# Q's and K's projections: weight columns streamed head by head, or with the two heads of a pair interleaved

## The chip, the cores and the metric

The kernel runs on one core of one Trainium2 chip. The core has a matrix engine (TensorE, "PE" in the profile, with its weight loads shown apart as "PEld"), a vector engine (DVE), a scalar engine (ACT), a GpSimd engine (POOL) and DMA queues that SyncE (SP) issues. Two memories on the chip matter here: SBUF, which holds operands, and PSUM, eight banks into which TensorE writes its products in float32. Both have 128 partitions. The metric is the time of one execution on the device, in microseconds (us). Before the change it was 845.99 us, the median of two runs (844.23 and 847.74).

## The reference

The input x has 2048 rows of 512. The output is a gated mix `g * a + (1 - g) * b`, where `g = sigmoid(sum(x * gate_w))`, `b` is a layer norm followed by a two-layer MLP with GELU (512 to 1376 to 512), and `a` is a recurrent attention over 64 segments of 32 rows, in order:

```
mem = mem0                                    # 8 rows of 512
for s in range(64):
    h = concat([mem, x[32*s : 32*s+32]])      # 40 rows
    q, k, v = h @ Wq, h @ Wk, h @ Wv          # 32 heads of 128 each
    p = softmax(mask(q @ k.T * scale))        # per head, 40 x 40
    o = (p @ v) @ Wo                          # back to 512
    mem = o[:8];  out[s] = o[8:]
```

Segment s+1 needs the memory rows that segment s ends with, so the segments form one chain from first to last.

## The kernel before, in words

The MLP runs first (lines 290 to 519, about the first 114 us of the span) and writes its part, already multiplied by `1 - g`, to DRAM. Then a loop of 64 segments follows (lines 600 to 669). Instructions stand in the order in which they are written: each engine works its own list from front to back, under a schedule that is written out by hand (`manual_schedule`).

A segment has 8 memory rows and 32 new rows. 24 of the new rows travel with the memory rows as a block of 32 rows (`hT`, three buffers used in turn). The other 8 rows of each of four segments are gathered into a second block of 32 rows (`GL`), and what is computed from it is computed ahead, for a tile T of four segments, in the gaps of earlier segments. The code calls these "left".

**The projections.** `qk_unit` (line 106) issues four matmuls for one of the four 128-row chunks `kc` of the model width. Each has 32 stationary columns (the 32 rows of the block) and streams 512 moving columns out of the weight matrix. The four, j = 0 to 3, go to four 32-column strips of the array (`tile_position=(0, 32 * j)`) and write the four groups of 32 partitions of one PSUM bank, so they run side by side; the text calls four such matmuls a quad. Strip j streams elements 32j to 32j+31 of each of 16 heads. A bank holds half of the heads (`hf`) of Q (`t` = 0) or K (`t` = 1), and takes four quads, 16 matmuls. A segment has four such banks `U[0]` to `U[3]` (Q and K, both halves, lines 615 to 623), 64 matmuls, and then V's eight quads (`v_unit`, line 126) into `X1` and `X2`.

`qk_cast` (line 112) turns a bank on ACT from float32 into a bf16 tile `Tb`. In `Tb` the two heads of a pair lie interleaved, so that two bf16 numbers form one 32-bit word. `qk_tr` (line 117) then transposes 32-bit words in blocks of 32 x 32 on DVE, into `QT` and `KT` (or `QL` for the left rows of Q; `kl_tr`, line 121, writes `KL` for the left rows of K). `scores` (line 249) multiplies them: `scores(s, 0)` uses the first half of the heads, `scores(s, 1)` the second. In the loop the order on TensorE is: 64 matmuls for Q and K, four quads of V into X1, two quads of V into X2, both halves of the scores, the last two quads of V.

After the scores come the exponentials on ACT (lines 636 and 637), the sums on TensorE (`sums`, line 263), a reciprocal and a multiplication on DVE (lines 647 and 648), the product with V (`av`, line 271), a copy to `UT` on ACT (line 653), the product with Wo (`wo_pass`, line 592, with line 140), a cast on ACT (line 596), a selection on TensorE (line 664) and the copy of the new memory rows into the next `hT` (line 665). Between these steps `run(n)` takes n quads from `side(T, si)`, the work for left rows. For `si` 0 and 1 these are the left rows of Q and K (`left_qk`, eight quads a segment), for `si` 3 those of V, for `si` 2 Wo of the left rows and the output. `W1`, `W2` and `W3` (line 599) set how many quads go into each gap: four before `av`, one after it, two after `wo_pass`, and the rest after line 664. `left_qk` hands its cast to a list `act_q` that is emptied behind the first bank of the next segment.

Of the kernel before, what the change touches and what calls it, by code (L numbers as in the profile page):

```python
# [27 lines left out]
def kernel(ctx, tc, A_x, A_mem0, A_Wq, A_Wk, A_Wv, A_Wo, A_seg_len, B_x, B_w1, B_b1, B_w2, B_b2, gate_w, out):  # L28
    nc = tc.nc
    P = 128  # L30
    _, S, Dm = A_x.shape
    H, Dh = A_Wq.shape[1], A_Wq.shape[2]
# [12 lines left out]
    NP = H // 2  # L45
# [12 lines left out]
    Wq_sb = pers.tile([P, KC, HD], BF16)  # L58
    Wk_sb = pers.tile([P, KC, HD], BF16)
# [37 lines left out]
    Sb = SbF[:, 0:NG * EW].rearrange("p (i c) -> p i c", c=EW)  # L97
    W = lps.tile([P, 512], FP32)

    Wq5 = Wq_sb[:].rearrange("p k (h j e) -> p k h j e", h=H, j=4)  # L100
    Wk5 = Wk_sb[:].rearrange("p k (h j e) -> p k h j e", h=H, j=4)
    W5 = (Wq5, Wk5)
    Wv5 = Wv_sb[:].rearrange("p k (i j e) -> p k i j e", i=NG, j=4)
    HF = ((0, H // 2), (H // 2, H))

    def qk_unit(bk, G, t, hf, kc):
        h0, h1 = HF[hf]
        for j in range(4):
            nc.tensor.matmul(bk[32 * j:32 * j + 32, :], lhsT=G[:, kc, :], rhs=W5[t][:, kc, h0:h1, j, :],  # L109
                             start=(kc == 0), stop=(kc == KC - 1), tile_position=(0, 32 * j))  # L110

    def qk_cast(bk):
        Tb = ew.tile([P, 8, 32, 2], BF16, tag="Tb", bufs=3, name="Tb")
        nc.scalar.copy(out=Tb[:].rearrange("p a e b -> p a b e"), in_=bk.rearrange("p (a b e) -> p a b e", a=8, b=2))  # L114
        return Tb

    def qk_tr(Tb, dst, hf):
# [52 lines left out]
    def left_qk(T, t, hf, bk):  # L170
        for kc in range(KC):
            qk_unit(bk, gl(T), t, hf, kc)
            if kc < KC - 1:
                yield
        def ca():
            Tb = qk_cast(bk[:])
            dve_q.append(lambda: qk_tr(Tb, QL[T % 2], hf) if t == 0 else kl_tr(Tb, T, hf))
        act_q.append(ca)
        yield
# [420 lines left out]
    for s in range(nseg):  # L600
# [14 lines left out]
        for n, (t, hf) in enumerate(((0, 0), (1, 0), (0, 1), (1, 1))):  # L615
            bk = U[n]
            for kc in range(KC):
                qk_unit(bk, hc, t, hf, kc)
            if n == 0:
                flush(act_q, 9)  # L620
            qk_tr(qk_cast(bk[:]), (QT, KT)[t], hf)
            if n == 0:
                flush(dve_q, 9)
# [209 lines left out]
```

## Time and profile before

| what | value |
|---|---|
| median of two runs | 845.99 us (844.23 to 847.74) |
| the profiled execution | 847.08 us, of which the span from first to last instruction 845.3 us |
| TensorE busy | 794.9 us (94%) |
| ACT busy | 559.5 us (66%) |
| DVE busy | 414.0 us (49%) |
| POOL busy | 252.2 us (30%) |
| granted TensorE clock, mean | 0.991 |
| line 109, Q and K matmuls | 4096 from `hT`, 1024 from `GL` |
| line 114, casts of Q and K | 258 from `U`, 62 from `X` |

Busy time is the time in which an engine has at least one instruction running. Matmuls are pipelined and their ends are modelled by the profile, so one matmul's shown duration (about 379 ns for 512 columns) is longer than the spacing of two; the spacing of starts is what counts. The "chain" is the work that ended last, followed back from the last instruction to what released each step. In the groups, the columns are: line, engine, operation, output and input, partitions x elements and type, count, then the busy time and the mean duration of one in ns, then the idle time of that engine just before. In the timeline, the columns are the start, the length, the engine, the line, the operation, and how many instructions are merged.

### The profile page before, as it was taken

How to read it: one execution, taken by the hardware profiler on the slowest of the kernel's cores; microseconds unless marked ns; L12 is line 12 of the kernel's file. 1: busy time of each engine (PE TensorE's matmuls, PEld its weight loads, DVE VectorE, ACT ScalarE, POOL GpSimd, SP SyncE). 2: the span in 40 equal slices, each digit the busy share in tenths (PEclk: the TensorE clock that was granted, in tenths of full speed). 3: DMA queues.
4: the chain of work that ended last, by engine and by line, in shares of the span. 5: the costliest groups of instructions: out<-in, count | busy, mean ns of one | idle time of the engine just before them, and what ended most of it. 6: DMA issues, size and time to landing. Idle time of an engine off the chain costs nothing.

```text
span 845.3 us, 39489 instructions
## 1 busy us (share of the span) xinstructions
PE 794.9 (94%) x17629; PEld 418.6 (50%) x17657; DVE 414.0 (49%) x942; ACT 559.5 (66%) x1311; POOL 252.2 (30%) x378
## 2 busy tenths in 40 slices
PE   2989999999999999999999999999999999999886
PEld 1656644555444545444445554444545454444443
DVE  5556435454445455544545454445445544544444
ACT  1545676676767676767676776767676767676663
POOL 3000013333333333333323333332333233323331
PEclk9989999999999999999999999999999999999999
DMA  9973011212122111212121212121111212121111
GB/s 294 414 281 122 27 40 46 72 54 78 53 72 66 56 58 58 78 60 78 53 85 51 62 53 83 54 77 61 60 54 60 78 59 78 59 72 52 57 51 61
DMA packets 39001, 70.30 MB, mean 83 GB/s; under 512 B 4005, under 2 KB 29194, under 8 KB 37290
## 3 DMA queue, kind: packets, MB, share of 16 engines
q1 hardware_dynamic: 38698, 67.59, 23.2%
q8 instruction: 140, 2.29, 1.1%
q0 software_dynamic: 128, 0.13, 0.2%
q14 instruction: 35, 0.29, 0.1%
HBM read 59.06 MB, written 4.45 MB: 75 GB/s over the span
## 4 chain that ended last, share of the span: by engine, by line
PE 75%; DVE 11%; ACT 8%; issue 3%; DMA 2%; SPq 1%; POOL 0%; DVEq 0%; ACTq 0%
PE U L109 27%; PE W L140 15%; PE X L128 13%; ACT w L596 4%; DVE R L647 3%; PE U L278 3%; ACT UT L653 2%; PE SbF L254 2%; PE U L460 2%; PE X L140 2%; PE W L664 2%; DVE E L648 2%; PE X L109 1%; PE U L265 1%; DMA xt<-in_A_x_dram 1%
## 5 line engine op out<-in xcount | busy, mean ns | idle before, releaser
L114 ACT CAST Tb<-U 128x512 bf16<-128x512 f32 x258 | 186.7, 761 | 64.6 <-PE U L109 38.7
L588 POOL TENSOR_TENSOR UT<-XR,Rb 128x768 bf16<-128x768 bf16 x63 | 105.0, 1667 | 253.8 <-DMA Rb<-r_dr 209.8
L109 PEld LDWEIGHTS <-hT 128*32 128x32 bf16 x4096 | 103.9, 97 | 116.7 <-DVE hT L665 15.7
L109 PE MATMUL U<-Wq_sb,hT 128*32 128x512 bf16 x2048 | 133.3, 380 | 5.7 <-DVE rmin L666 3.5
L128 PE MATMUL X<-Wv_sb,hT 128*32 128x512 bf16 x2048 | 132.8, 379 | 0.0
L109 PE MATMUL U<-Wk_sb,hT 128*32 128x512 bf16 x2048 | 132.7, 379 | 0.0
L140 PE MATMUL W<-Wo_sb,UT 128*32 128x512 bf16 x2080 | 124.1, 380 | 6.2 <-ACT UT L653 1.2
L118 DVE STREAM_TRANSPOSE QT<-Tb 128x256 f32<-128x256 f32 x128 | 57.0, 446 | 129.8 <-ACT Tb L114 126.8
L582 POOL TENSOR_TENSOR racc<-racc,R 128x320 f32<-128x320 f32 x63 | 54.6, 867 | 218.6 <-DVE R L577 210.7
L577 DVE RECIPROCAL R<-SbF 128x256 f32<-128x256 f32 x63 | 110.3, 1750 | 0.3 <-PE SbF L268 0.3
L140 PEld LDWEIGHTS <-UT 128*32 128x32 bf16 x2080 | 56.1, 96 | 60.6 <-issue 22.3
L653 ACT CAST UT<-U 128x64 bf16<-128x64 f32 x252 | 35.3, 226 | 69.9 <-PE U L283 69.9
L665 DVE CAST hT<-W 128x32 bf16<-128x32 f32 x63 | 12.1, 192 | 135.8 <-PE W L664 135.8
L572 ACT CAST XR<-U 128x256 bf16<-128x256 f32 x252 | 78.4, 434 | 0.0
L128 PEld LDWEIGHTS <-hT 128*32 128x32 bf16 x2048 | 49.9, 96 | 41.7
L118 DVE STREAM_TRANSPOSE KT<-Tb 128x256 f32<-128x256 f32 x128 | 56.8, 444 | 26.2 <-ACT Tb L114 25.8
L647 DVE RECIPROCAL R<-U 128x64 f32<-128x64 f32 x63 | 35.1, 558 | 69.7 <-PE U L268 66.4
L596 ACT CAST w<-W 128x512 bf16<-128x512 f32 x65 | 38.1, 586 | 44.5 <-PE W L140 44.5
L460 PE MATMUL U<-w_sb,hTm 128*128 128x512 bf16 (+1 forms) x164 | 51.6, 394 | 2.2 <-DMA w_sb<-in_B_w_dram 1.6
L454 PEld LDWEIGHTS <-w_sb 128*128 128x128 bf16 (+1 forms) x352 | 35.2, 104 | 32.5 <-issue 16.8
L114 ACT CAST Tb<-X 128x512 bf16<-128x512 f32 x62 | 46.3, 746 | 5.4 <-PE X L109 2.2
L109 PE MATMUL X<-Wk_sb,GL 128*32 128x512 bf16 x496 | 43.5, 384 | 0.0
(135 smaller groups left out, 1100.9 us busy)
## 6 DMA issues: line engine op xcount, KB each, us to landing
Rb<-r_dr SPq DMA_DIRECT2D x63, 512.0 KB
Wq_sb<-in_A_Wq_dram SPq DMA_DIRECT2D x4, 1024.0 KB
Wk_sb<-in_A_Wk_dram SPq DMA_DIRECT2D x4, 1024.0 KB
Wv_sb<-in_A_Wv_dram SPq DMA_DIRECT2D x4, 1024.0 KB
Wo_sb<-in_A_Wo_dram SPq DMA_DIRECT2D x4, 1024.0 KB
VP<-VL SPq DMA_DIRECT2D x64, 64.0 KB
xt<-in_A_x_dram SPq DMA_DIRECT2D x16, 128.0 KB
c_dr<-ct SPq DMA_DIRECT2D x16, 128.0 KB
```

Source lines behind the costliest of these rows:

```text
L109: nc.tensor.matmul(bk[32 * j:32 * j + 32, :], lhsT=G[:, kc, :], rhs=W5[t][:, kc, h0:h1, j, :], start=(kc == 0), stop=(kc == KC - 1), tile_ ...
L114: nc.scalar.copy(out=Tb[:].rearrange("p a e b -> p a b e"), in_=bk.rearrange("p (a b e) -> p a b e", a=8, b=2))
L118: nc.vector.transpose(out=dst[:, 8 * hf:8 * hf + 8, 0:32, :].rearrange("p a r b -> p a (r b)").bitcast(FP32), in_=Tb[:].rearrange("p a e b ...
L128: nc.tensor.matmul(bk[32 * j:32 * j + 32, :], lhsT=G[:, kc, :], rhs=Wv5[:, kc, 4 * vb:4 * vb + 4, j, :], start=(kc == 0), stop=(kc == KC - ...
L140: nc.tensor.matmul(bk[32 * c:32 * c + 32, :], lhsT=U_[:, j, i, :], rhs=Wo_sb[:, 4 * i + j, :], start=(n == 0), stop=(n == NW - 1), tile_po ...
L460: nc.tensor.matmul(bp(blk, tt)[:], lhsT=hTm[blk % 2][:rows, fc, tt * P:(tt + 1) * P], rhs=w2_sb[:rows, fc, :], start=(fc == 0), stop=(fc = ...
L572: nc.scalar.copy(out=XR[:, j], in_=U[j][:, 0:NG * 40].rearrange("p (i q) -> p i q", q=40)[:, :, 8:40])
L577: nc.vector.reciprocal(out=R[:, 8 * NG:], in_=SbF[:, 0:32 * NG])
L582: nc.gpsimd.tensor_tensor(out=racc[:], in0=racc[:], in1=R[:], op=ALU.add)
L588: nc.gpsimd.tensor_tensor(out=UT[(s + 1) % 2][:].rearrange("p j i q -> p (j i) q")[:, :, M:32], in0=XR[:, :, 0:RIDE], in1=Rb[:, :, 0:RIDE] ...
L596: nc.scalar.copy(out=w[:], in_=W[:])
L647: nc.vector.reciprocal(out=R[:, 0:8 * NG], in_=U[0][:, 320:384])
```

## The change

Three lines of the set-up and one of the cast change. The views `Wq5` and `Wk5` of the weights now give, for strip j, the order (pair a, element e, head b of the pair) instead of (head, element): the weights stay where they are in SBUF, but the moving operand takes element e of the first head, element e of the second head, then element e+1 of the first, and so on. `HF` counts pairs instead of heads. The columns of the PSUM bank come out in that order, so the cast reads and writes in order. V's view (`Wv5`) and all else stay.

```diff
-    Wq5 = Wq_sb[:].rearrange("p k (h j e) -> p k h j e", h=H, j=4)
-    Wk5 = Wk_sb[:].rearrange("p k (h j e) -> p k h j e", h=H, j=4)
+    Wq5 = Wq_sb[:].rearrange("p k (a b j e) -> p k a e b j", b=2, j=4, e=32)
+    Wk5 = Wk_sb[:].rearrange("p k (a b j e) -> p k a e b j", b=2, j=4, e=32)
     W5 = (Wq5, Wk5)
     Wv5 = Wv_sb[:].rearrange("p k (i j e) -> p k i j e", i=NG, j=4)
-    HF = ((0, H // 2), (H // 2, H))
+    HF = ((0, NP // 2), (NP // 2, NP))
 
     def qk_unit(bk, G, t, hf, kc):
         h0, h1 = HF[hf]
         for j in range(4):
-            nc.tensor.matmul(bk[32 * j:32 * j + 32, :], lhsT=G[:, kc, :], rhs=W5[t][:, kc, h0:h1, j, :],
+            nc.tensor.matmul(bk[32 * j:32 * j + 32, :], lhsT=G[:, kc, :], rhs=W5[t][:, kc, h0:h1, :, :, j],
                              start=(kc == 0), stop=(kc == KC - 1), tile_position=(0, 32 * j))
 
     def qk_cast(bk):
         Tb = ew.tile([P, 8, 32, 2], BF16, tag="Tb", bufs=3, name="Tb")
-        nc.scalar.copy(out=Tb[:].rearrange("p a e b -> p a b e"), in_=bk.rearrange("p (a b e) -> p a b e", a=8, b=2))
+        nc.scalar.copy(out=Tb[:].rearrange("p a e b -> p (a e b)"), in_=bk)
         return Tb
```

## The prediction

> **What bounds the kernel now.** I read the page's chain first, to learn which engine sets the end, then the timeline of one segment, then the groups by form for the durations.
>
> ```profile
> PE 75%; DVE 11%; ACT 8%; issue 3%; DMA 2%; SPq 1%; POOL 0%; DVEq 0%; ACTq 0%
> ...
> L114 ACT CAST Tb<-U 128x512 bf16<-128x512 f32 x258 | 186.7, 761 | 64.6 <-PE U L109 38.7
> ...
> L109 PE MATMUL U<-Wq_sb,hT 128*32 128x512 bf16 x2048 | 133.3, 380 | 5.7 <-DVE rmin L666 3.5
> ```
>
> TensorE holds 75% of the chain, and the largest entry of the chain by line is L109, the Q and K matmuls, with 27%. The L114 casts are not in the chain by name, though they are ACT's largest group. So the edit touches two things of unlike weight: the matmuls that bound the kernel, and a cast beside them. The timeline of a segment without Q/K left work (TensorE, and the last K transposition on DVE):
>
> ```profile
> 429.83 1.05 PE L109 MATMUL U<-Wq_sb,hT 128*32 128x512 bf16 x16
> 430.71 1.04 PE L109 MATMUL U<-Wk_sb,hT 128*32 128x512 bf16 x16
> ...
> 433.30 1.47 PE L128 MATMUL X<-Wv_sb,hT 128*32 128x512 bf16 x24
> 434.59 0.27 PE L254 MATMUL SbF<-QT,KT 128*32 128x40 bf16 x16
> 434.70 0.20 PE L258 MATMUL SbF<-QT,KL 128*32 128x64 bf16 x4
> 434.82 0.28 PE L254 MATMUL SbF<-QT,KT 128*32 128x40 bf16 x16
> ```
> ```profile
> 434.32 0.45 DVE L118 STREAM_TRANSPOSE KT<-Tb 128x256 f32<-128x256 f32 x1 [0.37 <-ACT Tb L114]
> ```
>
> The 64 matmuls start at 429.83 and V's first at 433.30: 3.47 us (3.46 in the segment from 406.93 to 410.39, which I use), or 0.216 us for a quad, 54 ns a matmul. V's 24 take 1.29 us to the next start, 54 ns too. A quad streams four times 512 columns in 0.216 us, so any change in how fast columns come reaches the time directly.
>
> The last K transposition ends at 434.77, and the second half of the scores starts at 434.82. The first half's L258 had started at 434.70, and a quad of 64 columns takes 0.03 us (the same quad at 434.94 is followed by V's at 434.96). So about 0.09 us of every segment is a wait for the last cast and transposition, although TensorE shows no idle time there.
>
> **Part one, the cast.** Rows by form:
>
> ```profile
> L596 ACT CAST w<-W 128x512 bf16<-128x512 f32 x65 | 38.1, 586 | 44.5 <-PE W L140 44.5
> ...
> L124 DVE STREAM_TRANSPOSE KL<-Tb 128x128 f32<-128x128 f32 x64 | 19.9, 391 | 3.0 <-ACT Tb L114 3.0
> ...
> L118 DVE STREAM_TRANSPOSE QL<-Tb 128x256 f32<-128x256 f32 x32 | 13.0, 405 | 7.2 <-ACT Tb L114 7.2
> ...
> L409 DVE TENSOR_TENSOR nt<-rs 128x2 f32<-128x2 f32 x24 | 3.9, 161 | 0.8
> ```
>
> L596 is the same cast in order, 512 float32 of PSUM to bf16: 586 ns. The 320 L114 casts (761 and 746 ns) should become that, some 171 ns less each, 55 us of ACT's 559.5 us. Nearly all of it lies beside TensorE's next quads. What reaches the path is the 0.09 us above, since the last cast's saving of 0.17 us is larger than that wait: 64 x 0.09 = 5.8 us gained. Behind it the exponential (L636) waits for the scores, with ACT idle 0.23 us ahead of it, so it does move up.
>
> **Part two, the moving operand.** No instruction is added, no DMA, no wait; the 5120 L109 matmuls read in another order. Before, a strip reads runs of 32 neighbouring elements (64 bytes). After, it alternates between two places 256 bytes apart and moves on by 2 bytes every second element. No matmul in this trace reads like that. The nearest on TensorE is L258, whose elements are 4 bytes apart, at the full rate (a quad of 64 columns in 0.03 us, by starts). That is one end: no cost. The nearest row with a wide step is on another engine: L124 writes words 512 bytes apart, L118 in runs. With the 161 ns of L409's two elements as the fixed part, L118 costs (405 - 161) / 256 = 0.95 ns a word and L124 (391 - 161) / 128 = 1.80 ns: 1.9 times. With the extreme durations of these groups (375 and 421 ns for L124, 401 and 446 for L118, the latter also into QT) it is 1.5 to 2.2 times. The worst end: the four strips of a quad take turns. One 512-column matmul alone takes 0.216 us (two of L460 take 0.43 in the chain), so a quad would take 0.864 us, 4 times.
>
> I take 2 times: the widest-step row gives 1.9, and a stream that loses one turn per element loses a whole one.
>
> [...]
>
> Path at 2 times. Main banks: 3.46 us more a segment, x 64 = 221.4 us, all on the chain. Left banks: eight quads in each of 30 segments (si 0 and 1, T + 1 from 1 to 15). They sit in gaps:
>
> ```profile
> 402.11 0.62 PE L109 MATMUL X<-Wq_sb,GL 128*32 128x512 bf16 x8
> 402.84 0.28 PE L278 MATMUL U<-E,V 32*128 32x40 bf16 x16
> ...
> 403.24 0.40 PE L109 MATMUL X<-Wk_sb,GL 128*32 128x512 bf16 x4
> 403.72 1.91 PE L140 MATMUL W<-Wo_sb,UT 128*32 128x512 bf16 x32
> ...
> 405.63 0.62 PE L109 MATMUL X<-Wk_sb,GL 128*32 128x512 bf16 x8
> 406.32 0.26 PE L664 MATMUL W<-SelM,w 128*128 128x8 bf16 x4
> ```
>
> From start to the next start less 0.216 us a quad, the free time is 0.30 us before L278 (four quads lie ahead of it), 0.26 before L140 (one), 0.26 before L664 (two), and 0.21 before the next segment (one quad from 406.50, L109 at 406.93). Doubled quads need 0.86, 0.22, 0.43 and 0.22 more; what sticks out is 0.56 + 0 + 0.17 + 0 = 0.73 us, x 30 = 21.9 us. The other 64 left matmuls run in the MLP's last block, 16 quads x 0.216 = 3.5 us. The cast gives back 5.8 us, since the cover of the last cast (six quads of V) does not change.
>
> Sum: 221.4 + 21.9 + 3.5 - 5.8 = 241.0 us, on the profiled execution's 847.08: 1088 us. That execution was 1.1 us over the median; I say **1087 us**, +28%.
>
> **Rivals.**
> *The strips also take turns (4 times).* For it: four streams at once now ask for a new place with every column. Against it: in the old order four strips together cost no more than one L460 matmul, and L258's four strips neither. Main 64 x 10.38 = 664.3; left, the four gaps need 2.59, 0.65, 1.30 and 0.65 more, 4.16 us net, x 30 = 124.8; first block 10.4; cast -5.8: 1641 us. Anything between 2 and 4 belongs here. [...]
> *The feed keeps its rate (not slower).* If whatever feeds a strip holds both places between accesses, or fetches fast enough for any step, part two is nothing and only the cast counts: 847.1 - 5.8 = 841 us, and no more, since the scores cannot start before the first half's L258 is through. The point is a quad of 0.222 us: above it the main banks' 64 x 16 quads lose more than the 5.8 us. For it: L258 at a step of 4 bytes. Against it: L124, and ACT's own L114, whose writes 4 bytes apart take 761 instead of 586 ns.
> *The cast doesn't get shorter.* Then each number is 5.8 us higher; it changes no verdict.
>
> **Numbers.** 0.58 for a loss of 1.5 to 2.2 times a quad; 0.22 for strips hindering each other as well; 0.16 for the full rate; 0.04 for something between or beyond. The first case's low end at 1.5 times: 110.7 + 3.9 + 1.7 - 5.8 = 110.5 us, 957 us. The range takes that and the turns' full price: 955 to 1640 us, which leaves out the full-rate case. A change under 2% (17 us) is hardly told from none here, so the full-rate case counts as "same": 0.13, with 0.03 for faster, should the cast free more than I see, and 0.84 for slower.
>
> **What would show it.** Right: starts of two L109 banks in a segment 1.73 us apart instead of 0.87; L109's share of the chain near 40%; L114 at about 586 ns; V's and Wo's quads still at 0.216 us; the granted clock as before; DVE and ACT idle longer ahead of L118 and L114. Wrong: banks 0.87 us apart (the feed does not mind), or 3.5 us (turns). A quad price that differs between Q and K, or between main and left banks, would say that the places in SBUF matter and not the step.

## The result, and the profile after

With the change an execution takes 1160.5 us (1160.03 and 1160.97), against 845.99 us before: 1.371 times as long, with a 95% interval of 1.367 to 1.375. The span of the profiled execution is 1159.2 us against 845.3, 313.9 us more. It was predicted to be slower, 1087 us in a range of 955 to 1640; the direction and the range held, and the loss was 73 us larger than the sum.

The page of the changed kernel: the chain by engine and by line, then the groups (line, engine, operation, count, busy us, mean ns, idle us before).

```profile
PE 89%; DVE 6%; ACT 3%; DMA 1%; issue 1%; SPq 0%; DVEq 0%
PE U L109 43%; PE X L109 11%; PE W L140 10%; PE X L128 10%; PE U L278 2%; ACT w L596 2%; PE U L460 2%; PE X L140 2%; PE SbF L254 1%; PE W L664 1%; PE U L265 1%; DVE R L647 1%; PE W L454 1%; DMA xt<-in_A_x_dram 1%; ACT UT L653 1%
...
L114 ACT CAST Tb<-U 128x512 bf16<-128x512 f32 x258 | 151.2, 586 | 361.6 <-PE U L109 361.1
L109 PE MATMUL U<-Wq_sb,hT 128*32 128x512 bf16 x2048 | 269.1, 644 | 1.4 <-DVE hT L665 1.1
...
L128 PE MATMUL X<-Wv_sb,hT 128*32 128x512 bf16 x2048 | 133.8, 379 | 0.0
```

The cast did what its edit says: 586 ns instead of 761. But ACT now stands idle for 361 us ahead of it, waiting for L109. L109 holds 43% of a longer chain, with another 11% for the left banks in X, where before it was 27% and about 1%. V's matmuls, whose view of the weights was not touched, took 133.8 us, against 132.8 before. So the loss is in Q's and K's matmuls. One segment on TensorE, with left work (the counterpart of the two timelines in the prediction):

```profile
571.13 2.11 PE L109 MATMUL U<-Wq_sb,hT 128*32 128x512 bf16 x16
573.07 2.10 PE L109 MATMUL U<-Wk_sb,hT 128*32 128x512 bf16 x16
...
578.86 1.47 PE L128 MATMUL X<-Wv_sb,hT 128*32 128x512 bf16 x24
...
580.25 0.20 PE L258 MATMUL SbF<-QT,KL 128*32 128x64 bf16 x4
580.28 0.31 PE L254 MATMUL SbF<-QT,KT 128*32 128x40 bf16 x16
...
583.28 0.27 PE L278 MATMUL U<-E,V 32*128 32x40 bf16 x16
...
584.17 1.90 PE L140 MATMUL W<-Wo_sb,UT 128*32 128x512 bf16 x32
...
587.15 0.25 PE L664 MATMUL W<-SelM,w 128*128 128x8 bf16 x4
...
587.83 2.10 PE L109 MATMUL U<-Wq_sb,hT 128*32 128x512 bf16 x16
```

A bank of 16 matmuls takes 1.93 us by starts (571.13 to 573.07 and on to 578.86), a quad 0.482 us instead of 0.216: 2.23 times. The four banks take 7.73 us instead of 3.47. The second half of the scores now starts 0.03 us after L258, where it was 0.12.

### The profile page after: what moved, and what is told of

Same layout as the page of the kernel before. It is cut to its first block, busy times and chain, and to the rows that moved or that the text cites. A ratio compares the mean times of both kernels' runs of the same rounds, so it can differ in the third digit from the quotient of the medians.

```text
span 1159.2 us, 39517 instructions
## 1 busy us (share of the span) xinstructions
PE 1122.0 (97%) x17657; PEld 413.7 (36%) x17657; DVE 417.4 (36%) x942; ACT 514.7 (44%) x1311; POOL 250.6 (22%) x378
## 4 chain that ended last, share of the span: by engine, by line
PE 89%; DVE 6%; ACT 3%; DMA 1%; issue 1%; SPq 0%; DVEq 0%
PE U L109 43%; PE X L109 11%; PE W L140 10%; PE X L128 10%; PE U L278 2%; ACT w L596 2%; PE U L460 2%; PE X L140 2%; PE SbF L254 1%; PE W L664 1%; PE U L265 1%; DVE R L647 1%; PE W L454 1%; DMA xt<-in_A_x_dram 1%; ACT UT L653 1%
## 5 line engine op out<-in xcount | busy, mean ns | idle before, releaser
L114 ACT CAST Tb<-U 128x512 bf16<-128x512 f32 x258 | 151.2, 586 | 361.6 <-PE U L109 361.1
L109 PE MATMUL U<-Wq_sb,hT 128*32 128x512 bf16 x2048 | 269.1, 644 | 1.4 <-DVE hT L665 1.1
L109 PE MATMUL U<-Wk_sb,hT 128*32 128x512 bf16 x2048 | 268.8, 644 | 0.0
L109 PEld LDWEIGHTS <-hT 128*32 128x32 bf16 x4096 | 105.3, 97 | 355.6 <-issue 339.4
L118 DVE STREAM_TRANSPOSE QT<-Tb 128x256 f32<-128x256 f32 x128 | 57.0, 445 | 265.9 <-ACT Tb L114 262.4
L128 PE MATMUL X<-Wv_sb,hT 128*32 128x512 bf16 x2048 | 133.8, 379 | 0.0
L140 PE MATMUL W<-Wo_sb,UT 128*32 128x512 bf16 x2080 | 123.8, 379 | 3.7 <-ACT UT L653 1.2
L118 DVE STREAM_TRANSPOSE KT<-Tb 128x256 f32<-128x256 f32 x128 | 57.0, 445 | 151.8 <-ACT Tb L114 151.8
L140 PEld LDWEIGHTS <-UT 128*32 128x32 bf16 x2080 | 54.3, 96 | 62.5 <-issue 22.3
L109 PE MATMUL X<-Wk_sb,GL 128*32 128x512 bf16 x496 | 75.9, 648 | 0.0
L109 PE MATMUL X<-Wq_sb,GL 128*32 128x512 bf16 x496 | 69.6, 644 | 0.0
L460 PE MATMUL U<-w_sb,hTm 128*128 128x512 bf16 (+1 forms) x176 | 54.6, 395 | 1.3 <-DMA w_sb<-in_B_w_dram 1.3
L114 ACT CAST Tb<-X 128x512 bf16<-128x512 f32 x62 | 36.5, 589 | 31.6 <-PE X L109 31.6
```

Of the source, the lines that this page charges most:

```text
L114: nc.scalar.copy(out=Tb[:].rearrange("p a e b -> p (a e b)"), in_=bk)
L118: nc.vector.transpose(out=dst[:, 8 * hf:8 * hf + 8, 0:32, :].rearrange("p a r b -> p a (r b)").bitcast(FP32), in_=Tb[:].rearrange("p a e b ...
L140: nc.tensor.matmul(bk[32 * c:32 * c + 32, :], lhsT=U_[:, j, i, :], rhs=Wo_sb[:, 4 * i + j, :], start=(n == 0), stop=(n == NW - 1), tile_po ...
L460: nc.tensor.matmul(bp(blk, tt)[:], lhsT=hTm[blk % 2][:rows, fc, tt * P:(tt + 1) * P], rhs=w2_sb[:rows, fc, :], start=(fc == 0), stop=(fc = ...
```

## The experiments

Each kernel ran next to the kernel before. Where no interval is given, the time is that of one execution, and the reading rests on the spacing of starts in its trace, which is the same in each segment.

### The cast alone

The matmuls as before, only the cast in order:

```diff
-        nc.scalar.copy(out=Tb[:].rearrange("p a e b -> p a b e"), in_=bk.rearrange("p (a b e) -> p a b e", a=8, b=2))
+        nc.scalar.copy(out=Tb[:].rearrange("p a e b -> p (a e b)"), in_=bk)
```

> The matmuls read as before the change; only the cast copies in order. The columns then reach Tb with the two heads of a pair not interleaved, so the scores mix other elements; the work is the same. Theory: the cast is worth 0.09 us a segment, the wait of the second half of the scores for the last transposition: 840 us (0.7% faster than before), L114 at 586 ns, the second L254 group 0.03 us after L258 instead of 0.12. Rival: the cast lies wholly beside other work: 846 us, ratio 1.000.

Measured: 843.14 us against 847.02, a ratio of 0.9957 (0.9940 to 0.9973). L114 fell to 586 ns. The timeline of one segment on TensorE:

```profile
556.63 0.20 PE L258 MATMUL SbF<-QT,KL 128*32 128x64 bf16 x4
556.66 0.31 PE L254 MATMUL SbF<-QT,KT 128*32 128x40 bf16 x16
556.79 0.22 PE L258 MATMUL SbF<-QT,KL 128*32 128x64 bf16 x4
```

The wait behind the first L258 is gone, as the theory said, so the cast was not wholly beside other work. It is worth less than the sum had it: the steps behind the wait each take about 0.01 to 0.02 us longer, so that from the first L258 to L265 it is 0.79 us (556.63 to 557.42) instead of 0.84 (434.70 to 435.54), and the segment (551.77 to 562.80) lasts 11.03 us instead of 11.09. From the loop's first matmul to the end it is 727.0 us (841.3 - 114.30) against 730.5 (845.3 - 114.76): 3.5 us, or 0.055 a segment, where 0.09 was expected.

### The moving operand alone

The matmuls as after the change, the cast as before it.

> The matmuls read as after the change; the cast writes at a 4-byte step as before it (so Tb gets the two heads in another order, and the scores mix other elements). Theory: the whole loss is the matmuls': 1160 us as with the change, or up to 6 us more; a bank of 16 matmuls takes 1.93 us by starts. Rival, that part of the loss comes from the two together: clearly under 1150 us.

Measured: 1160.57 us. Its groups:

```profile
L109 PE MATMUL U<-Wq_sb,hT 128*32 128x512 bf16 x2048 | 269.1, 644 | 1.4 <-DVE hT L665 1.1
...
L114 ACT CAST Tb<-U 128x512 bf16<-128x512 f32 x258 | 190.2, 737 | 328.8 <-PE U L109 328.4 <-ACT ct L466 0.4
```

L109's busy time is the changed kernel's to the tenth, with the slow cast beside it. The whole loss is the matmuls'. That the total is no larger than with the change is the first stage's doing: the loop starts at 116.63 us here and at 119.75 in the trace of the change. From there to the end it is 1042.2 us against 1039.5, so the fast cast is still worth 2.7 us.

### One strip of four

Is it the strips that hinder each other, or does each pay alone? Only strip 0 reads interleaved:

```diff
+    W6 = [W_[:].rearrange("p k (a b j e) -> p k a e b j", b=2, j=4, e=32) for W_ in (Wq_sb, Wk_sb)]
...
-            nc.tensor.matmul(..., rhs=W5[t][:, kc, h0:h1, j, :],
+            nc.tensor.matmul(..., rhs=W6[t][:, kc, h0 // 2:h1 // 2, :, :, j] if j < 1 else W5[t][:, kc, h0:h1, j, :],
```

> Only strip 0 of each quad reads with the two heads interleaved; strips 1 to 3 read runs of 32 elements; the cast copies in order (strips 1 to 3 so arrive not interleaved, and the scores mix other elements there). Theory A, each strip pays on its own: a quad takes as long as its slowest strip, between 0.43 and 0.48 us, so 1070 to 1155 us; a value below 0.48 gives the part of the 2.23 times that the four strips add to each other. Theory B, the strips share one feed and the penalties add up: a quad of 0.216 + 0.067 = 0.28 us, about 912 us.

Measured: 1160.23 us, as with four strips. The added line moves the matmuls to line 110. The timeline on TensorE:

```profile
558.11 0.40 PE L110 MATMUL U<-Wq_sb,hT 128*32 128x512 bf16 x3
558.58 0.64 PE L110 MATMUL U<-Wk_sb,hT 128*32 128x512 bf16 x1
558.59 0.40 PE L110 MATMUL U<-Wq_sb,hT 128*32 128x512 bf16 x3
559.06 0.64 PE L110 MATMUL U<-Wk_sb,hT 128*32 128x512 bf16 x1
```

One matmul of each quad is shown with 0.64 us, the other three with 0.40. The three even belong to a later bank: the strips drift apart, then all go on at the pace of the slow one, which comes every 0.48 us. So a strip alone needs 0.48 us for 512 interleaved columns, and three more interleaved strips add nothing to that. The rival in which the strips take turns is out, in part as well as in whole: all of the 2.23 times is one strip's own rate.

### How many elements in a row

Now the moving operand takes r neighbouring elements from each of 16 heads in turn, places 256 bytes apart; the cast is in order. The edit, with r = 1, 2 and 4 (32 is the kernel with the cast alone):

```diff
-    Wq5 = Wq_sb[:].rearrange("p k (h j e) -> p k h j e", h=H, j=4)
-    Wk5 = Wk_sb[:].rearrange("p k (h j e) -> p k h j e", h=H, j=4)
+    Wq5 = Wq_sb[:].rearrange("p k (h j e f) -> p k e h f j", h=H, j=4, f=r)
+    Wk5 = Wk_sb[:].rearrange("p k (h j e f) -> p k e h f j", h=H, j=4, f=r)
...
-            rhs=W5[t][:, kc, h0:h1, j, :]
+            rhs=W5[t][:, kc, :, h0:h1, :, j]
```

> The moving operand takes two neighbouring elements (4 bytes) from each of 16 heads in turn, places 256 bytes apart, then the next two; the cast copies in order (the scores mix other elements). [...] Theory B, each jump costs the same wherever it comes: half as many jumps as with the change, a quad of 0.216 + 0.267 / 2 = 0.35 us, about 840 + 137 + 11 = 988 us.

> The moving operand takes one element from each of 16 heads in turn (places 256 bytes apart), then the next element; the cast copies in order (the scores mix other elements). Against the change only the number of places differs, 16 instead of 2. [...] Theory C, with two places something of each is kept between accesses: more than 0.48 us a quad, so above 1200 us.

> Four neighbouring elements (8 bytes) from each of 16 heads in turn; the cast copies in order (the scores mix other elements). With two elements a quad took 0.43 us. [...] Theory B, each jump costs the same 2 columns that it cost with runs of two: a quad of 1.5 times, 0.33 us, about 965 us.

Measured: 1642.16 us with r = 1, 1098.08 with 2, 844.08 with 4. Banks on TensorE with r = 1, then 2, then 4:

```profile
554.82 3.62 PE L109 MATMUL U<-Wq_sb,hT 128*32 128x512 bf16 x16
558.25 3.62 PE L109 MATMUL U<-Wk_sb,hT 128*32 128x512 bf16 x16
```
```profile
560.05 1.92 PE L109 MATMUL U<-Wk_sb,hT 128*32 128x512 bf16 x16
561.78 1.92 PE L109 MATMUL U<-Wq_sb,hT 128*32 128x512 bf16 x16
```
```profile
553.42 1.04 PE L109 MATMUL U<-Wk_sb,hT 128*32 128x512 bf16 x16
554.29 1.04 PE L109 MATMUL U<-Wq_sb,hT 128*32 128x512 bf16 x16
```

The banks take 3.43, 1.73 and 0.87 us by starts. A bank is 4 x 512 columns of each strip, so a column costs 1.68, 0.845 and 0.42 ns; per place that is 1.68, 1.69 and 1.70 ns. **In all three runs a strip moved on to a new place every 1.68 to 1.70 ns**, four columns' time at the full rate (0.216 us / 512 = 0.42 ns). With four elements a place that is the full rate; with two a bank takes twice as long, with one four times. A jump that costs the same wherever it comes was expected to give 988 us with r = 2 and 965 with r = 4, and was wrong both times (1098.08 and 844.08). And r = 1 with 16 places, at 1642.16 us, is far worse than the change, which has two: the price that theory C gave, above 1200 us. That something of two places is kept, its reason, is not shown.

The trace with r = 1 also shows that this price did not follow TensorE's granted clock, which fell to 0.50 in some stretches of its loop. Two of them, first a bank of Q or K, then V's 24 matmuls (the columns: the stretch, its length, the busy time and count of PE, PEld, DVE, ACT and POOL, the granted clock, the DMA share, GB/s):

```profile
276.81:280.25 3.44, 3.44 (x22) 0.54 (x18) 0.45 (x1) 0.59 (x1) 0.00 (x0) 0.50 0.00 0
305.07:307.60 2.53, 2.53 (x28) 0.92 (x24) 0.45 (x1) 1.17 (x2) 0.00 (x0) 0.50 0.00 0
```

The bank keeps its 3.44 us at a clock of 0.50, where V's matmuls take 2.53 us instead of 1.32 (283.68 to 285.00, at a clock of 1.00). So in this run the time per place did not grow at half the clock; what sets it, and why the clock fell, stays open.

### How far apart, and how many places

Inside a head the step was made 8 and 16 bytes, and then two and four places were taken in turn (32 and 16 bytes apart). Q's and K's elements move alike, so the scores stay; the cast is the one before the change. Against the kernel before:

```diff
+    Wq5 = Wq_sb[:].rearrange("p k (h j c d) -> p k h d c j", h=H, j=4, d=4)     # step of 8 bytes; d=8: 16 bytes
...
+    Wq5 = Wq_sb[:].rearrange("p k (h j b e) -> p k h e b j", h=H, j=4, b=2)     # two places in turn; b=4: four
...
+            rhs=W5[t][:, kc, h0:h1, :, :, j]
```

The expectations call a stretch of 16 bytes a line; that this is the size that counts was the author's assumption when they were written, and the table below shows what the runs say of it.

> Inside each head the moving operand steps 4 elements (8 bytes) at a time, then starts again one element on; cast as before the change. Q and K permute alike, so the scores stay the same. Two accesses in a row fall into a 16-byte line, the next line is its neighbour. Theory A, only the hits in a line count: as runs of two, 0.43 us a quad, about 1100 us. Theory B, the distance counts, and neighbouring lines stream: 0.216 us, 846 us.

> Inside each head the moving operand steps 8 elements (16 bytes) at a time; cast as before the change; scores the same. One access a line, neighbouring lines. Theory A, only the hits in a line count: 0.48 us a quad, 1160 us. Theory B, the distance counts: 0.216 us, 846 us.

> Inside each head the moving operand alternates between two places 32 bytes apart, element by element; cast as before the change; scores the same. [...] Theory H, one of two alternating lines is held, whatever their distance: 0.48 us a quad, 1160 us. Theory D, only the distance of 256 bytes makes it so: 0.86 us a quad and 1640 us, or 0.22 us and 846 us.

> Inside each head the moving operand takes one element from each of four neighbouring 16-byte lines in turn; cast as before the change; scores the same. [...] Theory H3, half of the accesses always hit: 0.48 us, 1160 us.

| moving operand | accesses in a row to 16 bytes | bank, us | kernel, us |
|---|---|---|---|
| runs of 4, 256 bytes apart | 4 | 0.87 | 844.08 |
| runs of 2, 256 bytes apart | 2 | 1.73 | 1098.08 |
| step of 8 bytes | 2 | 1.73 | 1098.44 |
| one element, 16 places 256 bytes apart | 1 | 3.43 | 1642.16 |
| step of 16 bytes | 1 | 3.43 | 1638.84 |
| four places in turn, 16 bytes apart | 1 | 3.43 | 1642.55 |
| two places in turn, 32 bytes apart | 1 | 1.93 | 1159.01 |
| two places in turn, 256 bytes apart (the change) | 1 | 1.93 | 1160.5 |

Of what was expected, the step of 8 bytes came out as theory A (0.43 us a quad) and the step of 16 bytes as neither theory (1638.84 us, where 1160 or 846 was said); two places came out at theory H's 0.48 us a quad, four at 0.86 us, not at H3's 0.48.

The distance did not matter here: steps of 8 bytes cost as runs of two 256 bytes apart (1.73 us a bank), steps of 16 bytes as single elements 256 bytes apart (3.43 us). What the banks follow is how many accesses in a row stay within 16 bytes. With blocks of 32 bytes the step of 16 bytes would have cost what the step of 8 does, and with blocks of 8 bytes the step of 8 what the step of 16 does. Nor is it the length of the view's innermost dimension: that is 4 for the runs of 4, for the step of 16 bytes and for the four places, and their banks take 0.87, 3.43 and 3.43 us. The two-place order is the exception, at either distance. It costs 0.943 ns a column, 0.56 of the 1.68 ns that single elements cost otherwise; with four places in turn a column costs the full 1.68 ns (3.43 us a bank). The runs show these prices only: that one of two alternating places is held, as theory H has it, is not shown, and why two are cheaper than four stays open.

### Interleaving the weights once, in SBUF

If the loss is the order in which SBUF is read, the weights themselves could be interleaved once: the strips then read runs of 64 elements and the cast still copies in order. The raw weights of Q and K are loaded into the room of Wo and Wv, 32 copies of 1024 elements interleave them during the MLP, and Wv and Wo are loaded behind them. (The branch for a failed range test reads the weights by the same new layout.)

```diff
+    Wq5 = Wq_sb[:].rearrange("p k (a j e) -> p k a j e", a=NP, j=4)
...
+        def pair_up():
+            m = len(pieces)
+            D_, R_, kc, a = pieces.pop(0)
+            (nc.gpsimd if m % 2 else nc.vector).tensor_copy(
+                out=D_[:, kc, 256 * a:256 * a + 1024].rearrange("p (a d b) -> p a b d", b=2, d=Dh),
+                in_=R_[:, kc, 256 * a:256 * a + 1024].rearrange("p (a b d) -> p a b d", b=2, d=Dh))
...
+            if n >= 24 and pieces:
+                pair_up()
```

> The two heads of a pair are interleaved once in SBUF: 32 copies of 1024 elements on GpSimd and VectorE by turns, during the MLP; Wv and Wo are loaded after that. The matmuls then read runs of 64 elements (128 bytes), and the cast copies in order, with the reference's result. Theory: quads at 0.216 us, the cast's 4 us kept (as in the kernel with the cast alone, 843.1 against 847.0), if the copies lie beside the MLP's matmuls: 843 us. Rival: the copies delay the MLP's VectorE work by more than 4 us: above 847 us.

Measured: 862.38 us against 844.91, a ratio of 1.0196 (1.0169 to 1.0223). The loop kept the cast's gain: from its first matmul at 134.31 us to the end at 861.0 it takes 726.7 us, 3.8 less than before. But it starts 19.5 us later. VectorE's timeline, with GpSimd's first copies below:

```profile
29.46 0.16 DVE L420 SCALAR_TENSOR_TENSOR nt<-nt,ve 128x2 f32<-128x2 f32 x1
29.65 1.15 DVE L421 SCALAR_TENSOR_TENSOR rs<-nt,rs 128x2 f32<-128x2 f32 x1
30.84 1.20 DVE L419 TENSOR_TENSOR nt<-rs 128x2 f32<-128x2 f32 x1
```
```profile
29.51 5.04 POOL L323 COPY Wk_sb<-Wv_sb 128x1024 bf16<-128x1024 bf16 x4 [21.07 <-DMA Wv_sb<-in_A_Wk_dram]
```

Beside GpSimd's first copies, VectorE's L419 to L421, each on two elements, take 1.15 to 1.21 us instead of 0.16, about as long as one of GpSimd's copies (5.04 us for four). (Not every short operation does: L455, also on two elements, took 0.15 us at 38.62 us, beside a later copy.) L419 to L421 form the MLP's serial chain for the reciprocal root, which TensorE's next block needs; from 30 to 60 us TensorE is busy 15.5 us, against 26.0 before. So GpSimd's copies were taken away:

> As the kernel with the weights interleaved in SBUF, but in 64 copies of 512 elements, none on GpSimd: about 50 on VectorE in blocks 2 to 6 of the MLP, behind its own work for the block, and 14 on ACT; the reference's result. In the kernel before this one, VectorE's two-element operations took 1.2 us instead of 0.16 us while GpSimd copied, and the segments began 19.5 us later. Theory: without GpSimd's copies the MLP keeps its time within 1 or 2 us, and the loop keeps the cast's 4 us: 842 to 845 us. Rival: VectorE and ACT have no room for 33 us of copies in the MLP: above 849 us.

```diff
-            (nc.gpsimd if m % 2 else nc.vector).tensor_copy(
+            (nc.scalar.copy if on_act else nc.vector.tensor_copy)(
...
+            if 2 <= blk <= 6:
+                for _ in range((0, 0, 0, 0, 0, 0, 0, 3, 3, 3, 1)[fc]):
+                    pair_up(False)
+                if fc in (1, 3, 5):
+                    pair_up(True)
```

Measured: 862.4 us against 846.87, a ratio of 1.0194 (1.0167 to 1.0220). The loop again takes 726.8 us (860.2 - 133.36), and again starts late. The timeline in one of the MLP's blocks (L453, L454 and L466 are L442, L443 and L455 of the kernel before):

```profile
61.54 0.20 ACT L454 ACTIVATE th<-z_all 128x2 f32<-128x2 f32 x1 [3.39 <-DVE junk L453]
61.65 0.46 ACT L466 ACTIVATE hTm<-SbF,b_sb 128x256 bf16<-128x256 f32 x1
...
62.16 1.01 PE L465 MATMUL SbF<-yT,w_sb 128*128 128x256 bf16 x4 [2.92 <-ACT hTm L466]
```

On ACT `th` stands ahead of the GELU (L466) and ran ahead of it, at 61.54 and 61.65 us: `th` waits 3.39 us for VectorE (0.65 at 59.25 us in the kernel before), which is late by its copies, and TensorE waits 2.92 us for the GELU behind it. In the chain that ended last, ten of VectorE's copies stand in each of four blocks, with 3.38 or 3.39 us, 13.5 of the 18.6 us by which the loop starts later. The 30 us from 60 to 90, in this kernel and then in the kernel before (columns as above):

```profile
60.00:90.00 30.00, 23.54 (x145) 15.20 (x148) 19.34 (x71) 16.00 (x34) 0.00 (x0) 0.89 0.17 49
```
```profile
60.00:90.00 30.00, 29.41 (x213) 20.21 (x216) 19.16 (x75) 17.98 (x40) 0.00 (x0) 1.00 0.38 117
```

TensorE does 145 matmuls instead of 213, and the granted clock is 0.89 instead of 1.00. Of the kernels that keep the reference's scores none was faster than the kernel before. The layout is worth the loop's 3.8 us, and these two ways of paying for it cost about 19 us.

## Why the prediction was right in direction and short in size

**What bounds the kernel: right.** L109's matmuls carried the loss, with nothing else in the chain to take it up. L109 is 43% of the chain in U and 11% in X; near 40% was named as the sign.

**Part one, the cast: right in its place, mis-sized.** The wait of the second half of the scores is what the cast sets, and it went. The term was 5.8 us; the cast alone measured 3.5 us in the loop and 3.9 us by the medians. The cast's own new length, 586 ns, was right; ACT's busy time fell by 44.8 us (559.5 to 514.7) where 55 was said: that figure added up durations, and before, those of the casts from U add up to 196 us (258 x 761 ns) where their busy time is 186.7.

**Part two, the step that failed: "I take 2 times".** The row it rested on, VectorE's L124 against L118, is a write on another engine; that it gave 1.9 is near, but no run ties the two together. The other reason given, one lost turn per element, was the author's estimate, and no run shows such turns: with one element from each of 16 places a column took four columns' time (1.68 ns against 0.42), not two. With two places it took 2.23 times (0.943 ns), and why less is not shown. So the size came near by luck as much as by reading. The rival that was given 4 times has its price in those 16 places (1642.16 us, where it said 1641), but not its reason in the change: with one strip of four interleaved the kernel took 1160.23 us, as with all four (1160.5), so the price there is not four strips taking turns. The full-rate rival fell with it: L258, its evidence, has four accesses in 16 bytes, and so do the runs of four, at 844.08 us.

**The sum, term by term.** Main banks: 64 x 4.26 = 272.6 us, where 221.4 was said (51 us of the miss). Left banks: from L265 to L278 +0.88 us, L283 to L140 +0.02, L140 to L664 +0.38, L664 to the next segment +0.07, by starts in this segment and in the one at 400 to 407 us before; 1.35 us x 30 = 40.5 us, where 21.9 was said. At the measured quad the prediction's own gaps would give 1.11 us, 33 us; so 11 us of this is the rate, and 7 us that the free time ahead of L278 and L664 was some 0.11 us shorter than read from the starts. First block: 5.0 us (the loop's start, 119.75 against 114.76) for 3.5. At the measured quad its 16 quads would give 4.3; the rest is not the change's for certain, since with the moving operand alone the loop started at 116.63. Cast: 0.06 us x 64 = 3.8 us back for 5.8. Together, as a balance of these two traces, 272.6 + 40.5 + 5.0 - 3.8 = 314.3 us, where the spans differ by 313.9.

**What would show it.** V's and Wo's quads stayed at 0.216 us, the granted clock at 0.993 (0.991 before), and Q, K, main and left banks have the same quad (0.48 us), so the step and not the place decides, as was named.

## What to carry to other kernels

Count the elements of a matmul's moving operand that lie in a row within 16 bytes: in these runs four bf16 elements or more kept the full rate (0.87 us a bank), two doubled the time (1.73), one made it fourfold (3.43; 1.93 where only two places alternate), at steps of 8 and 16 bytes as at 256. Other element types and runs of three were not run. An order that saves the evacuation a strided write cost far more here on the matmul's side: 171 ns a cast, most of it hidden, against 1.07 us on each bank of the engine that sets the end. And an engine with idle time was not free room here: GpSimd's copies, and VectorE's copies ahead of work that another engine's list waits for, both came out as TensorE waits (the loop started 19.5 and 18.6 us later).

## What the runs showed of the hardware that was not expected

Two places in turn cost 2.23 times the bank of runs (1.93 us against 0.864) and four places 3.97 times (3.43 us), with the same single access in a row to 16 bytes; for two places the distance (32 or 256 bytes) made no difference (1.93 us both). With one element from each of 16 places a bank took 3.44 us at a granted clock of 0.50, like the run's other banks (3.43 us), while V's 24 matmuls took 2.53 us instead of 1.32. With one strip of four interleaved the other three ran two or three quads ahead of it, into the next bank (at 558.58 us the slow strip still in K's, the others at 558.59 us in Q's), and then went on at its pace, 0.48 us a quad. VectorE's L419 to L421, on two elements, took 1.15 to 1.21 us instead of 0.16 while GpSimd copied 1024 elements at a time.
